# RWKV-6 attention with a gated FFN: one prefix matmul and two exps per unit in the last two super-blocks, permuted FFN units, last output in two halves

## The chip, the cores and the metric

The kernel runs on one core of a Trainium2 chip. Five engines work from their own in-order instruction queues and meet through semaphores: TensorE (PE, matmul), VectorE (DVE), ScalarE (ACT), GpSimd (POOL) and SyncE (SP, which here issues nearly all DMA transfers). The metric is the device time in microseconds (us); 0.5% of it is about 1.06 us.

## What is computed

An RWKV-6 recurrence feeds a gated FFN. B = 4 sequences, H = 8 heads, S = 768 steps, D = 48; then 3072 tokens, d_model = 384, d_ff = 1536.

```python
for t in range(S):                       # state: [B, H, D, D]
    y[:, :, t] = r_t . (state + (u * k_t) v_t^T)
    state = w_t[..., None] * state + k_t v_t^T
x   = y.transpose(0, 2, 1, 3).reshape(B * S, H * D)
xn  = x / sqrt(mean(x * x) + 1e-6) * rms_g
g   = xn @ w_gate
out = (g * sigmoid(g) * (xn @ w_val)) @ w_out          # [3072, 384] float32
```

## The kernel before, in words

**Tiling.** Time is cut into chunks of L = 128 steps, so each sequence has six. Six super-blocks (SB0 to SB5, index m) hold one chunk of each of the four sequences (index j, a *unit*: 128 time steps on the partitions, 384 = 8 x 48 columns). In a step name such as `rk.4.1`, the first number is m and the second j.

**Attention of a unit.** `ln` takes the logarithm of w. `cs` (`cs_mm`, L385) multiplies it by triangular masks: `mask_nge` gives minus the sum of the logs from the own step to the end of the chunk (for r), `mask_gt` gives the sum over the later steps (for k), each 128x384 in a PSUM bank of its own. `exp` (L394) exponentiates both banks in one instruction of 768 elements, and `rk` (L406) multiplies r and k by them. `tr` (PE, SB0 and SB1) or `trp` (a transposing DMA, later) transposes the result; `q` and `qm` (L431, L434) form the masked 128x128 products per head, `y` (L444, L447) multiplies them by v and adds the carried state. `st`, `sn`, `dk`, `dke`, `dm` carry the state on. On the side, POOL computes r*k*u (`ruk1` L472, `ruk2` L476), DVE sums it over a head (`bs` L479), POOL multiplies by v (`yd` L484), and `xa` (L488) adds it to y. `sq` and `rs` (L492, L497) give the RMS factor, `xn` applies it, and `xt`/`xe` (PE transposes and copy) or `xep` (a transposing DMA) lay x down with d_model on the partitions.

**FFN.** `gv` (L532) is one block of a gate (`g`) or value (`v`) product: three matmuls of 512 columns, or six of 256 in SB0 and SB1, where two units form a group. `si` is Silu on the gate block, `hm` (L540) the product with the value block, and `o` (L548) four matmuls of the output product; `oo` copies a finished unit out of PSUM and `od` writes its 128x384 fp32 rows to DRAM. There are twelve blocks of 128 FFN units; `wo[:, f]` has to hold the rows of w_out for block f.

**Weights.** Gate, value and w_out arrive in fp32, once, at the start: 12 loads of 128x768 (`ldw`) and 6 for w_out (`ldwo`, L332), all through seven staging buffers. Each is cast to bf16 in two steps of 384 columns (`wc` L358/L360, with rms_g as scale; `wco`). A load can be issued only when both casts have emptied its buffer. A w_out load brings 256 rows: partition p gets rows p and 128 + p of them, two pieces of 1536 bytes.

**Order.** `PLAN` is a flat list of steps, and the program is that list: each engine executes its steps in the order of the list, and nothing re-orders them. `@n` names a buffer of a ring or a PSUM bank, `/V`, `/A`, `/G` the engine (DVE, ACT, POOL) where there is a choice. ACT changes between two function tables: `tab.le` (ln, exp) at the start of a super-block's exp phase and `tab.si` (Silu) at its end. `warm` steps are matmuls on a constant that fill PE at the start; there are 24.

**What the start of the old order looks like.** SP loads w, k, r of units 0, 1 and 3, then v, and weights in between (w.1, w.3, k.1, w.0, r.0, r.1, k.0, v.0, v.1, gate weight, k.2, ...). All 24 weight casts are on DVE (12) and ACT (12). DVE begins `rk.0 rk.1 vc.0 wc bs.1 bs.0 qm.0 vc.1 qm.1 xa.1 xa.0`, POOL begins `ruk1.1 ruk2.1 ruk1.0 ruk2.0 yd.1 ruk1.2 yd.0`.

`inv_w` (L396) and `r_over_w` (L400) are in the file but no step calls them, and `ONE_SUM`, the tuple of super-blocks that `cs_mm` and `cs_exp` ask for, is empty:

```python
def inv_w(self, m):          # iw = exp(-lw) = 1 / w, all four units
    self.nc.scalar.activation(out=self.iw[:, self.slot["iw", m], :, :, :], in_=self.lw[:, self.slot["lw", m], :, :, 0:D], func=AF.Exp, scale=-1.0)
def r_over_w(self, m, j, eng):   # r = r * iw, in place
    ...
        out=r, in0=r, in1=self.iw[:, self.slot["iw", m], j], op=ALU.mult)
```

Of the kernel before, what the change touches and what calls it, by code (L numbers as in the profile page):

```python
# [24 lines left out]
def bc_mid(ap: bass.AP, n: int, axis: int = 1) -> bass.AP:  # L25
# [22 lines left out]
ONE_SUM = ()  # L48
# [36 lines left out]
    "st": ("st_mm", "stb", 2),  # L85
    "sn": ("st_add", "", 0),
# [7 lines left out]
    "od": ("o_dma", "", 0),  # L94
}
PLAN = """
tab.le.0 ld.0.1.w@0 ld.0.3.w ld.0.1.k@0 ld.0.0.w ld.0.0.r ln.0.1.1@0 ld.0.1.r ldu ln.0.3.1 ld.0.0.k ldg cs.0.3@0
ld.0.0.v@0 ln.0.0.1 ld.0.1.v cs.0.0@2 ldw.1.g@0 cs.0.1@4 exp.0.0 ruk1.0.1@0 ub@6 ld.0.2.k exp.0.1 rk.0.0@0
ldw.5.g@1 exp.0.3 rk.0.1 tr.0.0@7 ube/A ld.0.2.w ruk2.0.1 vc.0.0.1@0/V tr.0.1@6 ld.0.3.r ruk1.0.0@1 tre.0.1@0/A
wc.1.g.1/V ld.0.2.r ruk2.0.0 bs.0.1 tre.0.0/A ld.0.3.k q.0.1@2 yd.0.1@0 bs.0.0 ldw.2.g@2 q.0.0@4 qm.0.1@0  # L100
warm.0@6 ln.0.2.1 ld.0.2.v wc.5.g.1/A vc.0.1.1/V wc.1.g.0/A ldw.4.g@3 qm.0.0@1 st.0.1@7 cs.0.2@2 ruk1.0.2@0
ld.0.3.v y.0.1@4 exp.0.2 yd.0.0@1 y.0.0@5 ldw.0.g@4 xa.0.1@0 warm.1 ruk2.0.2 xa.0.0@1 warm.2 sq.0.1 ldw.2.h@5
rk.0.3@1 warm.3 wc.5.g.0/A rs.0.1 st.0.0@4 warm.4 tab.si.1 bs.0.2 ldw.0.h@6 tr.0.3@5 rk.0.2 yd.0.2@2 warm.5
sq.0.0 wc.4.g.1/V ruk1.0.3@1 warm.6 vc.0.2.1/V xn.0.1@0/A warm.7 wc.4.g.0/A ruk2.0.3 warm.8 ldw.4.h@0
tre.0.3@1/V warm.9 sn.0.1/A warm.10 wc.2.g.0/V rs.0.0 warm.11 ldw.1.h@1 xt.0.1@0 bs.0.3 warm.12 tr.0.2@1
xe.0.1@0/A sn.0.0/V yd.0.3@3 q.0.3@2 wc.0.g.0/A ldw.3.g@3 tre.0.2/V wc.2.h.1/A vc.0.3.1/V q.0.2@4 warm.13
xn.0.0/V wc.0.g.1/A qm.0.2@2 xt.0.0@7 warm.14 wc.2.g.1/A ldw.5.h@4 warm.15 xe.0.0/A ldw.3.h@2 wc.0.h.1/V
wc.2.h.0/V gv.0.0.2.g@0 qm.0.3@0 ldwo.3@5 y.0.2@1 wc.1.h.0/A st.0.2@7 warm.16 st.0.3@4 gv.0.0.0.g@5 wc.1.h.1/A
wc.3.g.0/V wc.3.g.1/A warm.17 ldwo.4@1 wc.4.h.1/V warm.18 gv.0.0.3.g@2 wc.0.h.0/V sn.0.2/A ldwo.0@3 xa.0.2@2
si.0.0.2@0 gv.0.0.4.g@3 wc.5.h.1/V ldwo.1@6 sq.0.2 y.0.3@7 gv.0.0.5.g@1 wc.3.h.1/V si.0.0.0@1 wc.4.h.0/V rs.0.2  # L110
warm.19 sn.0.3/V ld.1.3.w@1 warm.20 gv.0.0.0.v@0 xn.0.2@1/A wco.3.0/G xa.0.3@3 gv.0.0.5.v@5 sq.0.3 ldwo.2@0
hm.0.0.0@0 gv.0.0.1.v@4 si.0.0.3@2 wco.4.0/G ld.1.1.v@1 si.0.0.5@1 xt.0.2@7 warm.21 warm.22 wco.3.1/A warm.23
rs.0.3 gv.0.0.1.g@2 wc.5.h.0/A xn.0.3/V wco.1.1/V wco.0.0/A xt.0.3@0 gv.0.0.2.v@1 wco.0.1/V wc.3.h.0/V ldwo.5@5
xe.0.3/V gv.0.0.4.v@6 hm.0.0.5 gv.0.0.3.v@0 ld.1.1.r@1 xe.0.2/V si.0.0.1@1 gv.0.1.2.g@5 wco.2.1/A hm.0.0.3
ld.1.3.v gv.0.1.1.v@7 hm.0.0.1 si.0.0.4@2 gv.0.1.3.g@2 ld.1.1.k hm.0.0.2 si.0.1.2@1 gv.0.1.0.v@0 wco.1.0/A
ld.1.0.w gv.0.1.0.g@3 wco.5.0/V ld.1.2.w gv.0.1.5.v@1 hm.0.0.4 si.0.1.0@0 gv.0.1.2.v@4 vc.1.1.1@1/A wco.2.0/V
ld.1.1.w wco.4.1/V gv.0.1.1.g@5 hm.0.1.2 ld.1.0.k gv.0.1.5.g@3 hm.0.1.0 si.0.1.1@2 o.0.0.0@6 ruk1.1.1@0 ld.1.0.r
si.0.1.3@1 hm.0.1.1 gv.0.1.4.g@0 si.0.1.5@0 wco.5.1/G ld.1.3.r o.0.0.1 hm.0.1.5 si.0.1.4@2 gv.0.1.4.v@4 ld.1.3.k
vc.1.3.1/V tab.le.1 ruk2.1.1 o.0.0.2 ld.1.2.r gv.0.1.3.v@5 ln.1.1.1@1 oo.0.0@0/V ld.1.0.v o.0.1.0@7 ln.1.0.1
bs.1.1 hm.0.1.4 ln.1.3.1 cs.1.1@2 ruk1.1.0@1 ld.1.2.k o.0.1.1 ln.1.2.1 hm.0.1.3 cs.1.0@0 exp.1.1 ruk2.1.0  # L120
ld.1.2.v o.0.1.2 exp.1.0 rk.1.1@2 o.0.2.0@6 yd.1.1@4 cs.1.2@4 oo.0.1@1/A rk.1.0 dk.1@2 ruk1.1.3@0 exp.1.2
tr.1.1@3 ld.2.0.k@0 cs.1.3@0 dke.1@0 ruk2.1.3 tre.1.1@2/V o.0.3.0@7 exp.1.3 od.0.0 bs.1.0 o.0.3.1 vc.1.0.1/A
rk.1.3@0 ruk1.1.2@1 ld.2.1.v@0 tr.1.0@2 ld.2.1.k o.0.3.2 bs.1.3 dm.1.3/G tre.1.0/A rk.1.2 q.1.1@0 ld.2.0.r
dm.1.1/G vc.1.2.1/A q.1.0@2 qm.1.1@1 tr.1.2@4 oo.0.3@2/A ld.2.2.k dm.1.0/G tr.1.3@5 tre.1.2@0/A qm.1.0@2
ld.2.1.r yd.1.0@0 y.1.1@7 tre.1.3/A yd.1.3@1 od.0.3 xa.1.1@0 y.1.0@4 st.1.2@0 sq.1.1 st.1.0@1 xa.1.0@1
ld.2.1.w@0 q.1.2@2 rs.1.1 ld.3.1.r@1 sq.1.0 q.1.3@4 o.0.2.1 xn.1.1@0/V rs.1.0 qm.1.3@0 xt.1.1@7 o.0.2.2 dm.1.2/G
xn.1.0/A xe.1.1@1/A ruk2.1.2 xt.1.0@4 st.1.3@5 oo.0.2@0/A ld.3.1.k y.1.3@7 xe.1.0/V tab.si.2 gv.1.0.2.v@4
ruk1.2.0@0 xa.1.3@2 ld.2.3.v gv.1.0.0.g@6 sn.1.0 ruk2.2.0 bs.1.2 sq.1.3 gv.1.0.2.g@7 ld.2.2.w sn.1.2 si.1.0.0@0
gv.1.0.1.g@1 rs.1.3 qm.1.2@1 ld.2.2.r si.1.0.2@2 st.1.1@0 yd.1.2@2 gv.1.0.0.v@6 xn.1.3@1/A ld.2.3.w sn.1.3
gv.1.0.3.g@7 hm.1.0.0@1 y.1.2@5 ld.2.0.w si.1.0.3@1 gv.1.0.4.g@2 xa.1.2@3 si.1.0.1@0 ld.2.3.k gv.1.0.1.v@3  # L130
hm.1.0.2 sq.1.2 xt.1.3@5 gv.1.0.5.g@6 ld.2.3.r hm.1.0.1 si.1.0.4@2 rs.1.2 gv.1.0.5.v@7 xe.1.3/V ruk1.2.2@1
si.1.0.5@0 ld.2.2.v gv.1.0.3.v@1 tab.le.2 ld.3.2.w@1 ruk2.2.2 o.1.0.0@4 hm.1.0.3 gv.1.0.4.v@5 ln.2.0.4@0
ld.3.2.k sn.1.1 o.1.0.1 bs.2.2 bs.2.0 ruk1.2.1@1 hm.1.0.4 cs.2.0@2 cs.2.1@0 xn.1.2/G hm.1.0.5 exp.2.0 o.1.1.0@6
ld.2.0.v dk.2@5 exp.2.1 rk.2.0@1 ruk1.2.3@0 o.1.0.2 ld.3.0.w dke.2@1 rk.2.1 xt.1.2@7 cs.2.2@2 ld.3.1.v@1
ruk2.2.1 o.1.1.1 exp.2.2 oo.1.0@2/V cs.2.3@0 trp.2.0@1 xe.1.2/V ruk2.2.3 o.1.1.2 rk.2.2@0 exp.2.3 dm.2.0/G
bs.2.1 tab.si.3 gv.1.1.2.g@5 ld.3.2.r rk.2.3 yd.2.0@3 gv.1.1.1.g@4 si.1.1.2@1 gv.1.1.0.g@7 bs.2.3 dm.2.1/G
od.0.1 si.1.1.1@2 vc.2.0.4@0/V gv.1.1.1.v@2 yd.2.1@4 si.1.1.0@0 trp.2.1@2 gv.1.1.2.v@3 ruk1.3.1@1 gv.1.1.4.g@0
hm.1.1.1 hm.1.1.2 dm.2.2/G ld.3.1.w si.1.1.4@2 q.2.0@4 yd.2.3@0 q.2.1@2 ld.3.3.w gv.1.1.0.v@1 qm.2.0@2 yd.2.2@1
oo.1.1@1/A gv.1.1.3.g@7 ld.3.0.r qm.2.1@0 y.2.0@0 ruk2.3.1 ld.3.2.v gv.1.1.5.g@6 st.2.0@4 xa.2.0@0 q.2.2@2
hm.1.1.0 sq.2.0 sn.2.0 si.1.1.5@1 q.2.3@0 rs.2.0 gv.1.1.5.v@5 qm.2.2@1 si.1.1.3@0 ld.3.0.v dm.2.3/G st.2.3@4  # L140
st.2.2@6 tab.le.3 y.2.1@7 xn.2.0@0/G ld.3.3.v qm.2.3@2 ld.3.3.r ln.3.0.4@1 xa.2.1@1 y.2.3@2 y.2.2@3 ld.4.0.r@0
xa.2.3@2 st.2.1@7 gv.1.1.3.v@0 xa.2.2@3 sq.2.3 ld.3.3.k o.1.2.0@1 sn.2.1 sq.2.2 rs.2.3 sn.2.3 cs.3.3@2 ld.3.0.k
dk.3@7 rs.2.2 sn.2.2 xn.2.3@1/A gv.1.1.4.v@4 sq.2.1 xn.2.2/V hm.1.1.3 xep.2.1@0 dke.3@0 rs.2.1 hm.1.1.4
vc.3.0.4@1/A cs.3.1@6 o.1.3.0@0 xn.2.1/V hm.1.1.5 xep.2.0 o.1.3.1 exp.3.1 o.1.2.1 exp.3.3 rk.3.1@2 cs.3.0@4
ld.4.2.v@0 ruk1.3.0@0 o.1.3.2 exp.3.0 rk.3.3@0 cs.3.2@6 dm.3.3/G o.1.2.2 od.1.1 exp.3.2 rk.3.0 st.3.3@2 dm.3.2/G
st.3.1@3 ld.4.0.v tab.si.4 sn.3.3 st.3.0@4 gv.2.0.3.g@5 dm.3.0/G od.1.0 rk.3.2 gv.2.0.1.g@2 ruk2.3.0 trp.3.0@0
bs.3.1 gv.2.0.5.g@6 si.2.0.1@0 ruk1.3.2@1 gv.2.0.3.v@7 si.2.0.3@2 gv.2.0.1.v@2 trp.3.1@1 oo.1.3@1/A ruk2.3.2
gv.2.0.2.g@5 hm.2.0.1@0 dm.3.1/G gv.2.0.11.g@0 hm.2.0.3 ld.4.0.w@0 oo.1.2@2/A gv.2.0.5.v@2 bs.3.2 si.2.0.5@1
gv.2.0.2.v@1 sn.3.0 si.2.0.11@0 ruk1.3.3@1 ld.4.3.v hm.2.0.5 gv.2.0.4.g@7 si.2.0.2@2 bs.3.0 ruk2.3.3
gv.2.0.8.g@6 ld.4.0.k si.2.0.4@1 sn.3.1 gv.2.0.4.v@0 hm.2.0.2 ld.4.3.k gv.2.0.0.g@4 hm.2.0.4 si.2.0.8@2 ld.4.1.v  # L150
q.3.0@2 bs.3.3 si.2.0.0@1 q.3.1@0 q.3.2@6 qm.3.0@0 ld.4.2.w gv.2.0.0.v@5 gv.2.0.7.g@4 ld.4.1.r qm.3.2@2 y.3.0@2
ruk1.4.0@0 gv.2.0.11.v@3 ld.4.3.w hm.2.0.0 gv.2.0.6.g@6 yd.3.0@2 ld.4.1.w hm.2.0.11 si.2.0.7@1 y.3.2@7
gv.2.0.9.v@5 qm.3.1@1 yd.3.2@3 si.2.0.6@0 od.0.2 gv.2.0.7.v@3 vc.4.0.4@0/A yd.3.1@4 xa.3.2@0 gv.2.0.6.v@4
# [42 lines left out]
class Env:  # L196
# [128 lines left out]
    def cast_w(self, g, w, q, eng):  # L325
        c, f = g // 2, g % 2 * (DF // 2) + q * DM
        dst = (self.wg if w == "g" else self.wv)[:, c, f:f + DM]
        src, sc = self.stage("stage", g, w)[:, q * DM:(q + 1) * DM], self.g_col[:, c:c + 1]
        self.scale(eng, dst, src, sc)
# [278 lines left out]
```

## Time and profile before

| what | value |
|---|---|
| median of 4 runs | 211.59 us (211.39 to 212.76) |
| the profiled execution's own time | 210.71 us |
| its span, first to last instruction | 208.9 us |
| PE busy (matmul) | 190.6 us, 1650 matmuls |
| DVE, ACT, POOL busy | 150.2, 129.5, 105.2 us |
| DMA | 36.74 MB, 130120 packets, mean 176 GB/s |
| TensorE clock granted | full in every slice |

Times in the profile's rows are those of one execution, counted from the start of its span. A duration of a row is one instruction's life; instructions of an engine overlap at their ends, on PE by half, so the distance between two starts is the cost where an engine is full. The chain of work that ended last is followed back from the last instruction to whatever released each step; a wait counts only where it lies on that chain. A landing is the time from issue to the end of a transfer.

### The profile page before, as it was taken

Reading aid. Unit: us, or ns where it says so; the run is one execution under the profiler, and the core shown is the slowest. Engines: PE = TensorE matmul, PEld = TensorE weight load, DVE = VectorE, ACT = ScalarE, POOL = GpSimd, SP = SyncE. Lnnn points to the kernel's source line nnn. Section 1 sums busy time; section 2 is a strip of 40 time slices with the busy share of each in tenths; the row PEclk is TensorE's granted clock in tenths of the full one; section 3 lists DMA queues with packets and bytes.
Section 4 is the critical chain, followed back from the end, with each engine's and each line's share of the span. In section 5 each row is a group of like instructions: output and inputs, shape, how many; then the busy total and the mean of one; then the engine's idle time right before and its main releaser. Section 6 shows DMA issues by size and latency. Waiting matters only on the chain.

```text
span 208.9 us, 4415 instructions
## 1 busy us (share of the span) xinstructions
PE 190.6 (91%) x1650; PEld 117.5 (56%) x1650; DVE 150.2 (72%) x251; ACT 129.5 (62%) x231; POOL 105.2 (50%) x135
## 2 busy tenths in 40 slices
PE   0668699999989999899999999999999999999991
PEld 0244477786769768775455565446654555444560
DVE  2277994877878799998697957799977965042721
ACT  4649867469788977698635976448875354333310
POOL 3176804047787599937919659445399522000000
PEclk9999999999999999999999999999999999999999
DMA  6999999999898979999999999999276007320033
GB/s 133 210 278 281 386 313 301 220 206 222 192 234 164 210 155 221 188 190 195 199 201 216 223 185 239 177 239 235 41 138 141 0 2 67 125 75 2 0 116 115
DMA packets 130120, 36.74 MB, mean 176 GB/s; under 512 B 123953, under 2 KB 128562, under 8 KB 130098
## 3 DMA queue, kind: packets, MB, share of 16 engines
q1 hardware_dynamic: 129696, 36.45, 79.0%
q8 instruction: 13, 0.21, 0.4%
q10 hardware_dynamic: 402, 0.00, 0.1%
q14 instruction: 9, 0.07, 0.1%
HBM read 25.96 MB, written 4.72 MB: 147 GB/s over the span
## 4 chain that ended last, share of the span: by engine, by line
PE 59%; POOL 11%; DVE 10%; DMA 7%; issue 6%; SPq 4%; ACT 3%; POOLq 0%; DVEq 0%; ACTq 0%
PE ps L532 34%; PE ps L548 17%; SPq L298 4%; POOL ruk L472 3%; DMA stage_x<-in_moe_w_out_dram 3%; POOL ydr L484 3%; DVE qts L434 3%; POOL ruk L476 2%; PE ps L385 2%; DVE rkA L406 2%; DMA in_w<-in_w_dram 2%; DMA in_rk<-in_k_dram 2%; PE ps L431 2%; POOL st L466 1%; PE ps L447 1%
## 5 line engine op out<-in xcount | busy, mean ns | idle before, releaser
L536 ACT ACTIVATE sg<-ps 128x512 bf16<-128x512 f32 x72 | 41.0, 595 | 41.3 <-PE ps L532 23.6
L540 DVE TENSOR_TENSOR ht<-ps,sg 128x512 bf16<-128x512 f32 x72 | 47.5, 683 | 17.2 <-PE ps L532 12.0
L532 PE MATMUL ps<-xnt,wv 128*128 128x256 bf16 (+1 forms) x288 | 55.0, 326 | 0.5 <-DVE wv L360 0.5
L532 PE MATMUL ps<-xnt,wg 128*128 128x256 bf16 (+1 forms) x288 | 54.8, 326 | 0.1
L548 PE MATMUL ps<-wo,ht 128*128 128x384 bf16 x288 | 53.8, 326 | 0.0
L472 POOL TENSOR_TENSOR ruk<-in_rk 128x384 f32<-128x384 f32 x24 | 24.3, 1012 | 34.7 <-DMA in_rk<-in_k_dram 12.0
L548 PEld LDWEIGHTS <-ht 128*128 128x128 bf16 x288 | 27.3, 98 | 18.0 <-issue 0.3
L532 PEld LDWEIGHTS <-wg 128*128 128x128 bf16 x288 | 27.3, 98 | 17.8 <-issue 0.4
L532 PEld LDWEIGHTS <-wv 128*128 128x128 bf16 x288 | 27.0, 98 | 17.6 <-DVE wv L360 0.8
L406 DVE TENSOR_TENSOR rkA<-in_rk,ps 128x768 bf16<-128x768 f32 x24 | 22.4, 949 | 10.6 <-ACT ps L394 10.6
L434 DVE TENSOR_TENSOR qts<-ps,mask_lt 128x1024 bf16<-128x1024 f32 x24 | 28.6, 1214 | 0.4 <-PE ps L431 0.4
L497 POOL TENSOR_TENSOR rstd<-rstd,mhalf 128x1 f32<-128x1 f32 x24 | 13.4, 563 | 23.6 <-ACT junk L492 23.4
L476 POOL TENSOR_TENSOR ruk<-ruk,u_bc 128x384 f32<-128x384 f32 x24 | 24.1, 1007 | 2.2 <-ACT u_bc L354 1.1
L394 ACT ACTIVATE ps<-ps 128x768 f32<-128x768 f32 x24 | 18.5, 795 | 6.2 <-PE ps L385 5.6
L484 POOL TENSOR_TENSOR ydr<-in_v,diag 128x384 f32<-128x384 f32 x24 | 20.4, 860 | 2.7 <-DVE diag L479 2.6
L466 POOL TENSOR_TENSOR st<-sf,wcr 128x384 bf16<-128x384 f32 x19 | 15.5, 832 | 1.9 <-ACT wcr L378 1.9
L488 DVE TENSOR_TENSOR xb<-ps,ydr 128x384 bf16<-128x384 f32 x24 | 13.0, 550 | 4.5 <-PE ps L447 2.4
L341 ACT ACT_TABLE_LOAD x12 | 15.4, 1283 | 0.9 <-PEq L592 0.7
L492 ACT ACTIVATE junk<-xb 128x388 bf16<-128x388 bf16 x24 | 12.6, 524 | 4.6 <-DVE xb L488 4.1
L350 DVE COPY obr<-ps 128x384 f32<-128x384 f32 x11 | 6.1, 553 | 12.1 <-PE ps L548 12.0
L385 PE MATMUL ps<-lw,mask_nge 128*128 128x384 bf16 x24 | 8.5, 355 | 6.5 <-ACT lw L344 6.4
L479 DVE TENSOR_REDUCE diag<-ruk 128x8 f32<-128x384 f32 x24 | 12.9, 544 | 0.4 <-POOL ruk L476 0.4
(71 smaller groups left out, 190.6 us busy)
## 6 DMA issues: line engine op xcount, KB each, us to landing
in_w<-in_w_dram SPq DMA_DIRECT2D x24, 192.0 KB, 3.7
in_rk<-in_k_dram SPq DMA_DIRECT2D x24, 192.0 KB, 3.7
in_rk<-in_r_dram SPq DMA_DIRECT2D x24, 192.0 KB, 3.9
in_v<-in_v_dram SPq DMA_DIRECT2D x24, 192.0 KB, 4.0
out_dram<-obr SPq DMA_DIRECT2D x24, 192.0 KB, 3.0
ht<-in_moe_w_gate_dram SPq DMA_DIRECT2D x5, 384.0 KB, 5.0
stage_x<-in_moe_w_val_dram SPq DMA_DIRECT2D x3, 384.0 KB, 4.8
ht<-in_moe_w_val_dram SPq DMA_DIRECT2D x3, 384.0 KB, 5.8
```

Source lines behind the costliest of these rows:

```text
L341: self.nc.scalar.preload_act_table_set(LN_EXP if kind == "le" else SILU)
L394: self.nc.scalar.activation(out=ps, in_=ps, func=AF.Exp)
L406: self.nc.vector.tensor_tensor(out=self.half("rkA", m, j)[:, :, :, 0:D], in0=self.in_rk[:, self.slot["in_rk", m], j], in1=self.b2(("cs", m ...
L434: self.nc.vector.tensor_tensor(out=self.qts[:, self.slot["qts", m, j]].rearrange("p a q t -> p (a q) t"), in0=self.b2(("qb", m, j)).rearra ...
L466: (self.nc.vector if eng == "DVE" else self.nc.gpsimd).tensor_tensor(out=self.st[:, m % 2, j].rearrange("p q (a d) -> p q a d", a=2), in0= ...
L472: self.nc.gpsimd.tensor_tensor(out=self.ruk[:, self.slot["ruk", m, j]], in0=rk[:, 0], in1=rk[:, 1], op=ALU.mult)
L476: self.nc.gpsimd.tensor_tensor(out=t, in0=t, in1=self.u_bc, op=ALU.mult)
L484: self.nc.gpsimd.tensor_tensor(out=self.ydr[:, self.slot["ydr", m, j]], in0=self.in_v[:, self.slot["in_v", m], j], in1=self.diag[:, m * SB ...
L532: self.nc.tensor.matmul(ps[:, a * n:(a + 1) * n].rearrange("p (u t) -> p u t", t=L), lhsT=w[:, c, f * 128:(f + 1) * 128], rhs=x[:, :, c], ...
L536: self.nc.scalar.activation(out=self.sg[:, self.slot["sg", m, g, i]], in_=self.b1(("gvb", m, g, i, "g")), func=AF.Silu)
L540: self.nc.vector.tensor_tensor(out=self.ht[:, self.slot["ht", m], fs[0]:fs[-1] + 1, t0:t0 + n], in0=self.b1(("gvb", m, g, i, "v")).rearran ...
L548: self.nc.tensor.matmul(ps, lhsT=self.ht[:, self.slot["ht", m], f, j * L:(j + 1) * L], rhs=self.wo[:, f, :], start=(f == 0), stop=(f == FC ...
```

## The change

1. `ONE_SUM = (4, 5)`: in SB4 and SB5 a unit has one prefix matmul (`mask_gt`) instead of two. `cs_exp` takes two exps of it, one with scale -1 and one with scale +1, 384 elements each. The first is the factor of r times w, so two new steps go with it: `iw` (`inv_w`, once per super-block, on ACT inside the exp phase) and `rw` (`r_over_w`, once per unit, in place in r, after `ruk1` of that unit has read it and before its `rk`).
2. The FFN units are permuted. A cast takes every second column of a staging buffer (384 of them, step 8 bytes), so that blocks of even and of odd units arise; partition p of a w_out load gets rows 2p and 2p + 1 of its 256, one piece of 3072 bytes; `cast_wo` puts the two halves at the matching blocks.
3. The last unit's output (`5.2`) is copied in two column halves, one by ACT and one by DVE, and written by two DMAs of 768-byte rows, one from ACT's queue and one from SP's.
4. `PLAN` is a new list. Every engine's order differs from the start on.

```diff
-ONE_SUM = ()
+ONE_SUM = (4, 5)
 OPS = {
+    "iw": ("inv_w", "iw", 1),
+    "rw": ("r_over_w", "", 0),
+    "ooh": ("o_out_half", "obr", 2),
+    "odh": ("o_dma_half", "", 0),
     def cast_w(self, g, w, q, eng):
-        c, f = g // 2, g % 2 * (DF // 2) + q * DM
-        dst = (self.wg if w == "g" else self.wv)[:, c, f:f + DM]
-        src, sc = self.stage("stage", g, w)[:, q * DM:(q + 1) * DM], self.g_col[:, c:c + 1]
-        self.scale(eng, dst, src, sc)
+        c, n = g // 2, DF // 2
+        dst = (self.wg if w == "g" else self.wv)[:, c, g % 2 * n:(g % 2 + 1) * n].rearrange("p (c i x) -> p c i x", c=2, x=128)
+        src = self.stage("stage", g, w).rearrange("p (i x c) -> p i x c", c=2, x=128)
+        self.scale(eng, dst[:, q], src[:, :, :, q], self.g_col[:, c:c + 1])
     def load_wo_hw(self, i):
-        self.nc.sync.dma_start(out=self.stage_o(i), in_=self.wout[i * 256:(i + 1) * 256, :].rearrange("(c p) m -> p c m", p=128))
+        self.nc.sync.dma_start(out=self.stage("stage_o", i), in_=self.wout[i * 256:(i + 1) * 256, :].rearrange("(p c) m -> p (c m)", c=2))
     def cast_wo(self, i, c, eng):
-        self.copy(eng, self.wo[:, 2 * i + c], self.stage_o(i)[:, c])
+        self.copy(eng, self.wo[:, i // 3 * 6 + c * 3 + i % 3], self.stage_o(i)[:, c])
+    def o_out_half(self, m, j, h):
+        x = slice(h * DM // 2, (h + 1) * DM // 2)
+        self.copy("DVE" if h else "ACT", self.obr[:, self.slot["obr", m, j], x], self.b1(("ob", m, j))[:, x])
+    def o_dma_half(self, m, j, h):
+        row0, x = j * 768 + m * L, slice(h * DM // 2, (h + 1) * DM // 2)
+        (self.nc.sync if h else self.nc.scalar).dma_start(out=self.out[row0:row0 + L, x], in_=self.obr[:, self.slot["obr", m, j], x])
```

The new order, by queue, at the places that matter:

```
start, SP:   w.0 k.0 w.1 r.3 r.1 w.3 k.1 v.1 [gate 2] r.0 w.2 r.2 v.0 k.3 [gate 1] [gate 0] [gate 5] [val 1] k.2 v.2 ...
start, DVE:  wc.2.g.1 ube rk.1 rk.0 bs.1 rk.3 bs.0 wc.1.g.1 qm.1 wc.5.g.0 xa.1 vc.0 qm.0 qm.3 rk.2 xa.0 tre.2 bs.3 wc.0.h.0 wc.2.h.1 wc.5.h.1 wc.3.g.0 xe.1 xe.0 ...
start, POOL: ruk1.0 ruk1.1 ruk2.0 ruk2.1 yd.0 yd.1 ruk1.3 rs.1 ruk2.3 wc.1.g.0 wc.5.g.1 yd.3 rs.0 wc.4.h.0 ruk1.2 ruk2.2 wc.2.h.0 ...
start, PE:   ... xt.0.0 warm x4 gv.0.0.5.g gv.0.0.4.g warm st.0.3 gv.0.0.3.g ...
SB4, ACT:    tab.le ln.4 iw.4 sq.3.3 exp.4.0 dke.4 exp.4.1 vc.4 exp.4.3 exp.4.2 tab.si
SB5, ACT:    tab.le ln.5 iw.5 sq.4.1 sq.4.2 sq.4.3 exp.5.3 xn.4.3 dke.5 oo.3.2 exp.5.2 oo.3.1 exp.5.1 exp.5.0 tab.si
end, PE:     gv.5.0.10.g gv.5.0.10.v o.5.1.0 gv.5.0.9.v o.5.3.0 o.5.1.1 o.5.0.0 o.5.1.2 ... o.5.2.2, then ooh x2, odh x2
```

Weight casts are now 10 on DVE, 10 on ACT and 4 on POOL (1.g, 5.g, 4.h, 2.h; `g` is gate, `h` is value). Of the eight `rw`, five are on DVE and three on POOL. SB0's u broadcast (`ube`) moves from ACT to DVE.

## The prediction, made before the changed kernel ran

> **What bounds the kernel now.** I first read busy time in stretches of the run (us, then busy us and instruction count by engine, granted clock, DMA share, GB/s).
>
> ```profile
> core 0: us, PE busy (x) PEld busy (x) DVE busy (x) ACT busy (x) POOL busy (x), PEclk, DMA share, GB/s
> 0.00:10.00 10.00, 3.81 (x8) 1.25 (x8) 2.13 (x11) 5.03 (x7) 3.00 (x13) 1.00 0.89 172
> 10.00:20.00 10.00, 7.59 (x63) 4.34 (x63) 7.51 (x12) 6.45 (x12) 6.94 (x8) 1.00 1.08 274
> 20.00:30.00 10.00, 7.80 (x84) 5.42 (x85) 10.00 (x19) 7.88 (x17) 4.74 (x6) 1.00 1.01 351
> ...
> 80.00:100.00 20.00, 18.61 (x221) 13.29 (x219) 18.18 (x27) 15.55 (x28) 14.76 (x19) 1.00 0.98 197
> 100.00:120.00 20.00, 19.81 (x167) 10.47 (x164) 17.30 (x28) 12.67 (x22) 12.59 (x15) 1.00 1.04 210
> 120.00:140.00 20.00, 20.00 (x141) 10.44 (x140) 15.38 (x25) 11.14 (x21) 12.41 (x14) 1.00 1.09 210
> 140.00:160.00 20.00, 20.00 (x193) 11.63 (x192) 16.80 (x28) 15.12 (x27) 13.54 (x17) 1.00 0.69 148
> ```
>
> There are two regimes. From 38 us TensorE (PE) is nearly full: idle is 0.54 us in 38-60, 0.46 in 60-80, 1.39 in 80-100, 0.19 in 100-120 and none afterwards, 2.6 in all. Before 38 us it is not. In 20-30 it seems 78% busy, but part of that is the `warm` filler (24 matmuls, 0.216 us each, 5.2 us together), and VectorE (DVE) has no gap. The clock is full throughout, so it plays no part. I then read the chain of work that ended last (start, duration, what).
>
> ```profile
> 29.46 0.67 DVE wv L360 x2
> 30.13 0.02 issue
> 30.14 6.46 DMA stage_x<-in_moe_w_out_dram
> 36.60 0.02 issue
> 36.62 0.63 DVE wo L350 x2
> 37.25 0.34 DVE wv L360
> 37.59 0.05 issue
> 37.64 7.27 PE ps L532 x65
> ...
> 198.17 6.51 PE ps L548 x40
> ...
> 204.75 0.48 ACT obr L354
> ```
>
> Up to 37.64 the chain is DMA and casts, then PE, then one output copy that ends at 205.23, and 3.7 us of writing out (span 208.93). The time is therefore (moment at which PE becomes full) + (PE work left) + (PE idle later) + (tail), and I cost the change in these four terms.
>
> **PE work.** SB4 and SB5 each lose four `mask_nge` prefix matmuls. In the timeline the two of a unit start 0.163 us apart (121.28, 121.45, 121.61), so eight give 1.30 us. They lie where PE is full (121-125 and 146-154), so all of it counts: **-1.30**. The group's mean of 355 ns must not be used: it is one instruction's life in an overlapped pipeline.
>
> **What SB4/SB5 pay for it.**
> - ScalarE (ACT): two `iw` of 1536 elements; nearest row is `ln` at 1.48 us. Eight units take two exps of 384 instead of one of 768: 2 x 0.48 (the 384-element PSUM copy) less 0.80, so +0.17 each. Together 4.3 us, half in each exp phase (table load to table load). SB4's phase also takes over a 1.47 us value cast. In the old SB4 phase (117.39-127.65) ACT idles 1.06 + 0.35, and 1.79 before its second silu: 3.2 us of cover against 1.48 + 0.68 + 1.47 = 3.6. SB5's phase idles 0.26 + 0.66 + 1.10 + 0.66 = 2.7 against 1.48 + 0.68 + one output copy 0.48 = 2.6. PE does not need ACT at once: the new plan gives it twelve `o` blocks (7.8 us), prefix and `dk` matmuls and five or six gate/value blocks (0.65 each) before it needs a silu, about 13 us, against my queue sums of 12 to 13 us for ACT. I take **0**; if the cover is gone it costs up to 1 us a phase.
> - `r/w`: five on DVE (0.55, the nearest row is the 384-element `st` multiply), three on POOL (1.01, the `ruk` row): 2.8 and 3.0 us. In 100-160 DVE idles 10.5 us of 60 and POOL 21. They must follow `ruk1` of their unit and precede `rk`; what waits behind a late one is `rk`, its exp banks and the next prefix matmul. **0**, bounds 0 and +1.
>
> **w_out in 3072-byte rows.** The Trainium skill (DMA: Bandwidth & Descriptors, Specifications) puts the least size for line rate at 512 B, so 1536 against 3072 B would be worth nothing. The trace disagrees:
>
> ```profile
> 22.00:24.00 2.00, 1.89 (x24) 1.14 (x22) 2.00 (x3) 1.70 (x4) 1.92 (x3) 1.00 1.03 396
> 24.00:26.00 2.00, 0.39 (x12) 0.23 (x8) 2.00 (x6) 1.63 (x3) 1.34 (x2) 1.00 1.05 412
> ...
> 30.00:32.00 2.00, 2.00 (x26) 1.72 (x24) 2.00 (x7) 1.50 (x4) 0.60 (x1) 1.00 0.90 300
> 32.00:34.00 2.00, 2.00 (x19) 1.69 (x18) 1.19 (x3) 1.81 (x5) 0.51 (x1) 1.00 0.84 270
> ```
>
> Gate and value weights (3072 B rows) move at 396-412 GB/s, w_out (1536 B) at 270-300. For the 2.36 MB of w_out that is 5.9 instead of 8.3 us, part of it only because the queue is less full (0.84-0.90). I use it: 1.05 us per w_out load instead of 1.4, so 1.3 to 2.4 us of queue time. On the path it is worth what the plan makes of it, below.
>
> **Permuted casts and the new start.** Weight casts now read every second fp32. On DVE, contiguous ones take 0.41; without the two-per-cycle mode I bound them by 0.61 (384 elements at the 1 ns slope between rows). The skill (VectorE: DVE Perf Modes, What auto-detection actually checks) makes that mode depend on memory and dimensions, not on step; I take 0.41. Four casts go to POOL, where no such row exists: its fp32-to-bf16 copy took 0.51, its bf16 tensor-scalar 1.255, and twice that, 2.5, if the wider strided source halves it. I take 1.25.
>
> The whole start is re-ordered, so I lay it out by queue. Loads landed at 3.6, then one per 0.9 us (192 KB) or 1.05 us (384 KB). In the new order r of unit 0 is tenth, behind one weight: 12.2 us (before it was fifth, 7.6). POOL then runs two `ruk1` and two `ruk2` at 1.0: 16.3. DVE, in order, waits for that: `bs`, `rk.3`, `bs`, cast, `qm` (0.47, 0.87, 0.47, 0.33, 1.15) to 19.6; cast and `y`, then `xa.0.1` to 20.7; `vc`, two `qm`, `rk.2`, `xa.0.0` (0.3, 2.3, 0.87, 0.47) to 24.7; `tre`, `bs.3` to 26.0. POOL meanwhile: `yd`, `yd`, `ruk1`, `rs`, `ruk2` to 23.2, two weight casts to 25.7, `yd.3` (waits for `bs.3`) to 26.8, `rs.0.0` to 27.4. Then `xn` 0.6, transposes 0.3, `xe` 0.35: the first gate matmul can start at 28.8, against 27.13 before, **+1.67**.
>
> From there, before: 61 of the 256-column matmuls at 0.109, 8 warms, two each of `y`, `st`, `xt`, and about 1.0 us of waiting, until 37.64. After: the same warms, one `y` and one `st` fewer (-0.37), and by my queue sums almost no waiting (-0.95): gates are cast by 30.8, values by 33, the three w_out casts on DVE wait for landings at 35 to 36, two blocks before PE needs the banks behind them. I reach twelve blocks at 39.2, where the old schedule would stand at 30.97 + 12 x 0.656 = 38.84: **+0.35**. The faster w_out rows are already in this; at 1.4 us a load those landings come 1 us later.
>
> **Later idle.** All the rest of the order is new too, and the 2.6 us of idle are a property of the old order. I found no stall by queue sums in the exp phases of SB4 and SB5. Nor is there one in the last twelve blocks: the last `hm` is ready 0.5 us before `o.5.1.2` needs it. For 38-120 I cannot say: **0**, with -2 to +2.
>
> **Tail.** The last copy becomes two of 192 columns on ACT and DVE: 0.35 (DVE's 0.55 less 192 elements at about 1 ns) instead of 0.48, **-0.13**. The store becomes two, on ACT's queue and SP's. The skill (DMA: Bandwidth & Descriptors, Issuing engines are not separate DMA queues) says both run on the same 16 engines and only issue time is saved: by that rule 0 of the 3.7 us. By the row, if the movement (192 KB at 300 GB/s, 0.6 us) were halved, -0.3. I take -0.12 between them, **-0.25** with the copy.
>
> **Sum.** 208.93 - 1.30 + 0.35 + 0 - 0.25 = 207.73 of span. The profiled execution took 210.71, 1.78 above its span: 209.5. The runs' median of 211.59 lies 0.88 above that execution: **210.4**.
>
> **Rivals.**
> - *The new order also removes idle.* The 1.39 us in 80-100 came from a late k load of SB3 (chain: landing at 95.5, `rk`, `st`), and SB3's loads are ordered anew; with -2 there the result is 208.4. For it: a single late load made most of it. Against it: POOL gets more work. 0.20.
> - *Slower: the POOL casts hold up the first FFN block.* `wc.1.g.0` and `wc.5.g.1` stand ahead of `yd.3` and `rs.0.0` on POOL, with 0.3 us of slack. At 2.5 us each they add 2.2 us to the start, PE has nothing but warms, and the result is 212.6; with strided DVE casts at 0.61 on the same path (five before `xe`), 213.4. The gain is eaten from 1.25 + (1.2 + 0.3)/2 = 2.0 us a cast. For it: DVE is busy throughout and the POOL rows next to busy DVE grow (1.18 for 1.00). 0.25.
> - *The matmuls go, but the time stays:* ACT's exp phases become the bound at 0.6 us each, or idle in 38-120 grows by 1.2: 211.6. 0.10.
> - Forecast, 210.4 with its own range 209.3-211.5: 0.45.
>
> About 0.5% (1.06 us: below 210.53, above 212.65) is what a measurement of this kernel can tell from no change. The forecast's own range falls a little over half below 210.53 (0.26); with the first rival 0.46 faster; the slower rival and the forecast's upper edge give 0.24 slower; 0.30 between. The range, 207.9 to 213.2, takes in both rivals' centres.
>
> **What would show it.** Right: 24 + 16 matmuls on the two prefix masks; the first L532 matmul near 28.8; w_out loads spaced near 1.05 us; POOL fp32 weight casts near 1.25; the exp phases longer by 2-3 us with PE at 20.00 of 20; the last copies near 0.35. Wrong: POOL casts above 2 us, the first gate matmul after 30 us, PE idle above 3 us between 40 and 120, or a first silu of SB3 or SB4 that PE waits for.

## The result, and the profile after

| | before | after |
|---|---|---|
| median | 211.45 us (63 runs) | 210.83 us (44 runs) |
| range | 209.88 to 213.89 us | 208.74 to 212.99 us |
| the profiled execution | 210.71, span 208.9 us | 211.20, span 209.3 us |

The ratio is 0.9954, 95% interval [0.994, 0.9968]: about 1.0 us faster, where the medians differ by 0.6 us and the forecast was 210.4. The ratio is of the means of the runs that lie within 1.5% of the fastest of their kernel, which leaves out 8 of the 44 of after and 3 of the 63 of before. The profiled execution of before lies 0.7 us below its median and that of after 0.4 above, so the two spans must not be subtracted. Differences of one part are taken from timed runs with intervals, and the traces only say where.

First the same stretches of the run as were shown of before (us, busy us and instruction count by engine, clock, DMA share, GB/s).

```profile
core 0: us, PE busy (x) PEld busy (x) DVE busy (x) ACT busy (x) POOL busy (x), PEclk, DMA share, GB/s
20.00:30.00 10.00, 6.61 (x82) 3.86 (x81) 8.67 (x16) 8.19 (x18) 7.02 (x8) 1.00 1.04 307
...
120.00:140.00 20.00, 20.00 (x155) 10.99 (x154) 16.56 (x29) 15.56 (x27) 12.85 (x15) 1.00 1.06 199
140.00:160.00 20.00, 19.98 (x178) 11.40 (x176) 17.81 (x30) 17.11 (x33) 17.55 (x21) 1.00 0.69 153
```

The two regimes are still there. In the exp phases of SB4 and SB5 (120 to 160) PE is full, though ACT has 32.7 us of work in them instead of 26.3. The start is thinner: VectorE is busy 8.67 us of 10 between 20 and 30 us, where it had no gap before. PE's idle time after 38 us is 3.3 us (0.71, 0.25, 0.90, 1.39 and 0.02 in the stretches from 38 on) against 2.6.

Next the chain of work that ended last, from the start of the second regime to the end.

```profile
28.60 6.00 DMA ht<-in_moe_w_val_dram
...
35.65 0.94 POOL ydr L489
...
205.88 0.37 DVE obr L355
206.25 0.02 issue
206.27 0.32 ACT obr L359
```

Where before a w_out load led to PE at 37.64, now a value weight that lands at 34.6 and POOL's `yd` of unit 0.2 do, and PE runs from 37.23 on. The two halves of the last output stand one behind the other.

Of the new work, the exp of 384 and the weight cast on POOL, in the groups by shape (instruction count, then busy us and mean ns):

```profile
L396 ACT ACTIVATE ps<-ps 128x384 f32<-128x384 f32 x8 | 3.8, 475 | 0.4 <-PE ps L390 0.2
...
L365 POOL TENSOR_SCALAR wg<-ht,g_col 128x384 bf16<-128x384 f32 x2 | 2.5, 1270 | 0.0
```

Those prices were met: the exp of 384 took 0.475 (forecast 0.48), `r/w` 0.56 and 1.10 (0.55 and 1.01), the weight cast on POOL 1.27 (1.25). A strided DVE cast took 0.42 where nothing lay beside it (forecast 0.41).

### The profile page after: what moved, and what is told of

Read it like the earlier page. It is cut to its first block, busy times and chain, and to the rows that moved or that the text cites. A ratio compares the mean times of both kernels' runs of the same rounds, so it can differ in the third digit from the quotient of the medians.

```text
span 209.3 us, 4422 instructions
## 1 busy us (share of the span) xinstructions
PE 187.9 (90%) x1642; PEld 116.4 (56%) x1642; DVE 149.4 (71%) x248; ACT 136.4 (65%) x244; POOL 116.7 (56%) x144
## 4 chain that ended last, share of the span: by engine, by line
PE 68%; DMA 8%; SPq 7%; DVE 7%; ACT 4%; issue 2%; POOL 1%; DVEq 0%; ACTq 0%; POOLq 0%
PE ps L537 39%; PE ps L553 20%; SPq L302 5%; DMA in_v<-in_v_dram 3%; DMA ht<-in_moe_w_val_dram 3%; DMA rkT<-rkA 3%; DVE qts L439 2%; PE ps L390 2%; PE ps L436 2%; DVE xb L493 2%; SPq L327 2%; DVE rkA L411 2%; PE ps L452 1%; PE ps L449 1%; ACT rkT L359 1%
## 5 line engine op out<-in xcount | busy, mean ns | idle before, releaser
L541 ACT ACTIVATE sg<-ps 128x512 bf16<-128x512 f32 x72 | 41.3, 598 | 33.2 <-PE ps L537 26.6
L537 PE MATMUL ps<-xnt,wv 128*128 128x256 bf16 (+1 forms) x288 | 55.9, 326 | 1.0 <-DVE xb L493 0.3
L537 PE MATMUL ps<-xnt,wg 128*128 128x256 bf16 (+1 forms) x288 | 53.7, 326 | 0.0
L502 POOL TENSOR_TENSOR rstd<-rstd,mhalf 128x1 f32<-128x1 f32 x24 | 13.9, 581 | 22.6 <-ACT junk L497 22.4
L471 POOL TENSOR_TENSOR st<-sf,wcr 128x384 bf16<-128x384 f32 x17 | 14.6, 867 | 4.4 <-ACT wcr L383 4.4
L359 ACT COPY obr<-ps 128x384 f32<-128x384 f32 (+1 forms) x15 | 7.0, 467 | 12.5 <-PE ps L553 9.9
L493 DVE TENSOR_TENSOR xb<-ps,ydr 128x384 bf16<-128x384 f32 x24 | 12.8, 550 | 3.2 <-POOL ydr L489 1.9
L399 ACT ACTIVATE ps<-ps 128x768 f32<-128x768 f32 x16 | 12.3, 794 | 2.7 <-PE ps L390 2.6
L349 ACT ACTIVATE lw<-in_w 128x384 bf16<-128x384 f32 (+1 forms) x12 | 9.8, 838 | 4.3 <-DMA in_w<-in_w_dram 4.3
```

Source lines behind the costliest of these rows:

```text
L471: (self.nc.vector if eng == "DVE" else self.nc.gpsimd).tensor_tensor(out=self.st[:, m % 2, j].rearrange("p q (a d) -> p q a d", a=2), in0= ...
L493: self.nc.vector.tensor_tensor(out=self.xb[:, self.slot["xb", m, j], 0:DM], in0=self.b1(("yb", m, j))[:, 0:DM], in1=self.ydr[:, self.slot[ ...
L537: self.nc.tensor.matmul(ps[:, a * n:(a + 1) * n].rearrange("p (u t) -> p u t", t=L), lhsT=w[:, c, f * 128:(f + 1) * 128], rhs=x[:, :, c], ...
L541: self.nc.scalar.activation(out=self.sg[:, self.slot["sg", m, g, i]], in_=self.b1(("gvb", m, g, i, "g")), func=AF.Silu)
```

## Experiments

Three measures from the traces recur below. **First gate matmul** is the start of the first `gv`. **Twelve blocks** is the start of the last of the 72 matmuls of 256 columns that make up the first twelve FFN blocks, plus its cost of 0.11 us. **Rest** is PE's end less that moment. Each is of one execution: the rest of after is 164.1 and that of the same kernel in the control 166.5, so differences of 2 us between two rests say nothing. Ratios are to the kernel before, timed alongside on the same chip.

### The new order with one part taken out

*Control: the kernel after as it is.*

> The changed kernel again, unaltered, for a second execution of it in the profile. Theory A (the start of the new order costs about 2.9 us, the rest gains it back): the first gate matmul lies at 29.5 to 30.5 us again, twelve FFN blocks are done at 41 to 42.5, the last PE instruction to the end of the span takes 3.3 to 3.6 us. Theory B (the profiled execution was an unlucky one and the start costs about 0.4 us as predicted): twelve blocks done at 39 to 40.

*Two prefix sums again, in the new order.*

```diff
-ONE_SUM = (4, 5)
+ONE_SUM = ()
 (PLAN: the two iw and eight rw steps are left out)
```

> The changed kernel with two prefix matmuls and one wide exp in SB4 and SB5 again, no iw, no r/w; everything else in the new order. If the eight matmuls lie on a full PE and nothing else there binds, it is 1.3 us slower than the changed kernel. If ScalarE's longer exp phases had eaten the gain, it is equal to it or faster.

*One copy and one store at the end.*

```diff
-ooh.5.2.1@0 ooh.5.2.0 odh.5.2.0 odh.5.2.1
+oo.5.2@0/A od.5.2
```

> The changed kernel with the last unit copied by ScalarE and stored by SP in one piece. By the prediction's tail term it is 0.25 us slower than the changed kernel. By the two traces alone (PE's end to span's end 4.25 us before, 3.45 after) 0.8 us slower. If the two halves only run one after the other, as the trace has them (0.36 and 0.32 us), and a transfer's end doesn't depend on its size, equal or up to 0.2 us faster.

*w_out in rows of 1536 bytes.*

```diff
-self.wout[i * 256:(i + 1) * 256, :].rearrange("(p c) m -> p (c m)", c=2)
+self.wout[i * 256:(i + 1) * 256, :].rearrange("(c p) m -> p c m", p=128)
```

> The changed kernel with w_out loaded in two pieces of 1536 bytes per partition again; the rows then lie in the wrong FFN blocks, so this part of the computation is changed, with the same instructions. If row length sets the rate (400 against 280 GB/s), the w_out loads take 0.4 us more each and 1 to 2 us more together, and the kernel is 0.5 to 1 us slower. If 512 bytes are enough for full rate, equal.

This run leaves out the matching of w_out rows to FFN blocks, so its output differs; the instructions are the same.

| run | median, us | ratio, 95% interval | first gate matmul | twelve blocks | rest |
|---|---|---|---|---|---|
| control | 212.55 | 0.9970 [0.9938, 1.0003] | 30.8 | 41.1 | 166.5 |
| two sums | 214.25 | 1.0057 [1.0021, 1.0092] | 30.7 | 41.8 | 167.4 |
| one store | 212.22 | 0.9968 [0.9932, 1.0005] | 30.7 | 41.1 | 163.9 |
| short rows | 212.70 | 0.9973 [0.9942, 1.0004] | 31.4 | 42.1 | 165.3 |

The single prefix sum is worth 1.0057 - 0.9970 = 0.87% or 1.85 us, with about 1 us on either side when the two intervals are combined. It carries the whole gain: with two sums the new order is 0.57% (1.2 us) slower than before. The halved store (0.9970 against 0.9968) and the long rows (0.9970 against 0.9973) are worth nothing that can be measured.

### The old order with one part put in

*The two halves alone; the permutation with the long rows alone.* The edits are the diff's own.

> The kernel before with the last output in two halves alone. Prediction's term: 0.25 us faster than before. Reading the two traces alone: 0.8 us faster. Halves one after the other and a transfer's end independent of its size: equal.

> The kernel before, in its own order, with the permuted FFN units and w_out in rows of 3072 bytes alone. If row length sets the rate, the w_out load that the chain waits for (issue 30.14, landing 36.6) lands about 1 us earlier, and the kernel is 0.3 to 1 us faster. If strided casts cost 0.2 us more each on VectorE (12 of them), the start is up to 2 us slower. If neither, equal.

*One sum in the old order.* The r*k products of units 4.3 and 5.0 had to come before their `rw`, so they moved ahead, into a third buffer.

```diff
-ONE_SUM = ()
+ONE_SUM = (4, 5)
 (PLAN, SB4)
-ln.4.0.4@0 ... exp.4.1 ruk1.4.1@1 rk.4.0@1 ... rk.4.1 ... exp.4.3 ... rk.4.2
+ln.4.0.4@0 iw.4@0 ... exp.4.1 ruk1.4.1@1 rw.4.0/V rk.4.0@1 ... rw.4.1/V rk.4.1 ... ruk1.4.3@2 rw.4.3/G exp.4.3 ... rw.4.2/V rk.4.2 ruk2.4.3
```

> The kernel before, in its own order, with one prefix matmul and two exps in SB4 and SB5 alone (the ruk steps of units 4.3 and 5.0 moved ahead of their rk, into a third buffer). If the eight matmuls are what counts: 1.3 us faster than before. If the order must be made anew to hide the longer exp phases: 0 to 1 us slower than before, with PE idle in 120-130 and 150-158.

*All three in the old order.*

> The kernel before, in its own order, with all three parts. Theory A (the new order's start costs 2.9 us, later idle gives back 0.4): the sum of the parts without that cost, 2 to 3 us faster than before and 1 to 2 us faster than the changed kernel. Theory B (the new order is neutral): about 1 us faster than before, equal to the changed kernel. If the exp phases bind in the old order: no faster than before.

*Only the moved products and the third buffer, with two sums.* This is the control of the one-sum run.

> The kernel before with two prefix sums in every unit, as it was, and only the two r*k products of units 4.3 and 5.0 moved ahead, into a third buffer, as the one-sum run in the old order had to have them. That run was 4.4% slower than before. Theory (the old order has no room on VectorE and ACT for the inverse, the r/w products and the second exp): this control is within 0.3% of before, ratio 0.998 to 1.003, and the 9.4 us belong to the new work. Rival (moving the products on GpSimd, and the sums that wait for them, did it): ratio 1.01 to 1.045.

| run | median, us | ratio, 95% interval |
|---|---|---|
| halves | 212.32 | 1.0004 [0.9977, 1.0031] |
| permutation and long rows | 212.56 | 1.0018 [0.9985, 1.0051] |
| one sum | 221.84 | 1.0443 [1.0394, 1.0492] |
| all three | 220.94 | 1.0376 [1.0326, 1.0425] |
| moved products alone | 212.42 | 0.9997 [0.9962, 1.0031] |

The halves and the rows are worth nothing here either. The surprise is the single sum, which takes eight matmuls away and costs 4.4% (9.4 us). The control with the moved products is at 0.9997, so the loss belongs to `iw`, `rw` and the second exp. The windows of the one-sum run say where it lies:

```profile
120.00:140.00 20.00, 16.52 (x100) 8.35 (x98) 14.31 (x22) 12.23 (x22) 13.34 (x14) 0.91 0.78 141
140.00:160.00 20.00, 18.98 (x186) 10.80 (x185) 17.72 (x30) 13.26 (x26) 7.35 (x10) 1.00 0.83 177
```

PE is idle 3.5 and 1.0 us in these stretches, where it was full before, and another 3.1 us from 160 to 180. The clock falls to 0.91 in the first: eight output matmuls that begin at 129.66, behind waits of 1.62 and 1.19 us, took 2.77 us instead of 1.46. The chain in SB5's exp phase shows the mechanism:

```profile
162.85 1.00 POOL in_rk L400
...
163.87 0.97 DVE rkA L404
...
168.07 5.93 DMA rkT<-rkA
```

`rw` (L400) and, from 160.51 on, the products that must precede it stand in front of `rk` (L404). `rk` frees the banks of the next prefix matmul (PE waited 5.0 us in four places for it) and releases the transposing DMA, which takes 5.9 us. `rw` is not alone in it: in SB4, `iw` on ACT stands in front of the square of another unit, and VectorE (2.6 us) and POOL (3.0 us) wait for what follows from that square. So `iw`, `rw` and the second exp are not separated here, and this is one placement of them in the old order; others were not tried. In the new order most `ruk1` and `rw` stand ahead of their exp, and PE has output and gate blocks queued in front of what needs them: in the trace of after it waits 0.7 us for `rk` from 38 to 160 us.

### The start of the new order

By then the start stood out as the mis-sized term: over the five traces of the new order above (after among them) the first gate matmul comes at 30.1 to 31.4 instead of 28.8 and the twelve blocks at 41.0 to 42.1 instead of 39.2. My theory was that late loads do it, the value weight of the chain above and r of unit 0.0.

*The late value weight issued earlier.*

```diff
-sq.0.0 wc.5.g.1/G ldw.4.h@1 ... wc.0.g.0/A ... ldw.3.h@2
+wc.0.g.0/A sq.0.0 wc.5.g.1/G ldw.3.h@2 ldw.4.h@1 ...
```

> The kernel after, with two steps moved in the start: the ACT cast that empties a staging buffer (gate weight 0, first half) ahead of the square of unit 0.0 that it stood behind, and the value weight 3 load, which waits for that buffer, ahead of the value weight 4 load. In the profile after, this load was issued at 28.60, landed at 34.6, and VectorE waited 2.91 us for it at 34.6. Theory (the start lost 1.8 us instead of the forecast's 0.35, and part of that is this late load): the load lands 2 to 4 us earlier, the wait is gone, the twelve blocks of the first FFN group are done 0.5 to 1.0 us earlier than after (41.6 in the mean of five runs of that order, so 40.6 to 41.1), and the ratio to before is 0.992 to 0.995 against 0.997. Rival (the whole weight stream limits, so another load becomes the late one, value weight 4 first): twelve blocks still at 41.3 to 42, ratio 0.996 to 0.999.

*In addition r of unit 0.0 two loads earlier, and the first weight cast on DVE behind `rk`.*

```diff
-ld.0.1.v@0 ldg cs.0.1@2 ldw.2.g@0 exp.0.1 ld.0.0.r ... wc.2.g.1/V ... ube/V rk.0.1@0 ruk1.0.0@0 ldw.1.g@1 rk.0.0
+ld.0.0.r ld.0.1.v@0 ldg cs.0.1@2 ldw.2.g@0 exp.0.1 ... ube/V ... rk.0.1@0 ruk1.0.0@0 ldw.1.g@1 rk.0.0 wc.2.g.1/V
```

> As the run before, and r of unit 0.0 is loaded two places earlier (ahead of v.1 and of the first gate weight), with the first DVE weight cast moved behind the two r, k products and the u copy ahead of it, so that neither GpSimd nor VectorE waits for that weight. Theory (the first gate matmul came at 30.1 to 31.4 instead of 28.8 because GpSimd's products started at 12.8 and VectorE had no gap from then on): r lands about 1.5 us earlier, VectorE's first head sum starts at 15.2 instead of 16.7, the first gate matmul at 28.6 to 29.5, the twelve blocks are done at 39.5 to 40.5, and the ratio to before is 0.986 to 0.991. Rival (the weight stream or VectorE's own sum of work decides the start): first gate matmul at 30 or later, ratio 0.994 to 0.998.

*In addition the last output product in two PSUM banks.*

```diff
+if (m, j) == (5, 2):   # per f and half h, 192 columns into bank 3 or 6
+    self.nc.tensor.matmul(self.last(h)[:, x], lhsT=..., rhs=self.wo[:, f, x], ...)
```

> As the run before, and the output product of the last unit is made in two column halves in two PSUM banks (24 matmuls of 192 columns instead of 12 of 384), so that the two copies of the tail need not run one after the other as they did after (VectorE 205.88 to 206.24, ACT 206.27 to 206.59). Theory (the forecast's 0.13 us for the copy were lost because ACT waited for VectorE): the two copies overlap, PE's end to the end of the span is 3.1 us instead of 3.45 to 3.5, PE's work grows by at most 0.3 us for the shorter matmuls, and the ratio equals the run before within 0.001. Rival (the stores alone set the tail): copies overlap but the tail stays at 3.4 to 3.6. The start is that of the run before in both, so its first gate matmul and twelve blocks are a second reading of it.

| run | median, us | ratio, 95% interval | first gate matmul | twelve blocks | rest |
|---|---|---|---|---|---|
| early value weight | 213.41 | 1.0050 [1.0013, 1.0086] | 30.7 | 42.2 | 166.4 |
| and early r | 213.53 | 1.0005 [0.9960, 1.0050] | 31.5 | 42.7 | 164.9 |
| and two banks | 213.06 | 1.0013 [0.9977, 1.0048] | 30.5 | 41.5 | 166.5 |

The theory fell. The value weight did come earlier and VectorE's 2.9 us of waiting for it were gone, but the kernel got no faster. r of unit 0.0 came 2 us earlier too (in the run with the early r, POOL's first product began at 10.71 instead of 12.78), and this is what VectorE did with it in the two-banks run, which has the same start:

```profile
14.36 0.55 DVE L479 TENSOR_REDUCE diag<-ruk 128x8 f32<-128x384 f32 x1 [0.89 <-POOL ruk L476]
16.93 0.95 DVE L406 TENSOR_TENSOR rkA<-in_rk,ps 128x768 bf16<-128x768 f32 x1 [2.02 <-DMA in_rk<-in_k_dram]
```

The number in brackets is the wait before the instruction. The first head sum starts 2.3 us earlier (14.36 for 16.66), and then VectorE waits 2.02 us for k of unit 0.3 and reaches that product at 16.93, where after reached it at 17.13. In the run with the early r it was 17.87, behind a wait of 2.62 us. That load has the same loads in front of it in both orders, only in another sequence, and the DMA engines have no free share here (1.02 and 1.04 in the windows of after). So the load that moved gains only until the next one that did not.

In the second half of the start, PE itself tells what it waited for. Between the first gate matmul and the twelve blocks the forecast has 10.4 us. The control and the one-store run take 10.3, without a wait; the other six take 10.7 to 11.7, with 0.2 to 0.9 us of waiting. First the wait of the run with the early value weight, then the last one of after:

```profile
36.34 1.38 PE L533 MATMUL ps<-xnt,wv 128*128 128x256 bf16 x11 [0.82 <-POOL wv L361]
```

```profile
37.23 0.81 PE L537 MATMUL ps<-xnt,wv 128*128 128x256 bf16 x6 [0.34 <-DVE xb L493]
```

In all three runs of this section PE waits once, for POOL's second value-weight cast (0.82, 0.76 and 0.60 us). Moving value weight 3 ahead made value weight 4 the late one: POOL's cast of it starts at 31.6, 32.1 and 30.9, and in the five other traces at 30.1 to 30.7. That is the rival of the expectation, though twelve blocks at 42.2 and a ratio of 1.005 are worse than it said. In after the 0.81 us are in part two casts (0.29 and 0.17), and the rest is `xa` of unit 0.2. POOL's rows of after show that unit's `yd`:

```profile
30.11 1.28 POOL L365 TENSOR_SCALAR wv<-ht,g_col 128x384 bf16<-128x384 f32 x1 [1.77 <-DMA ht<-in_moe_w_val_dram]
...
33.63 1.27 POOL L365 TENSOR_SCALAR wv<-ht,g_col 128x384 bf16<-128x384 f32 x1
35.65 0.93 POOL L489 TENSOR_TENSOR ydr<-in_v,diag 128x384 f32<-128x384 f32 x1 [0.75 <-DVE diag L484]
```

Two fp32 weight casts stand in front of it, but both were done at 34.9, and it waited another 0.75 us for its head sum, which stood in VectorE's queue behind the late value weight. So three different waits make up this half in the eight traces, each below 1 us. They do not explain all of the early value weight's 0.5%: its trace has 1.4 us more PE idle after 38 us than that of after, which I did not follow up.

The two banks did what was asked of the copies:

```profile
207.96 0.32 ACT L354 COPY obr<-ps 128x192 f32<-128x192 f32 x1 [2.07 <-PE ps L550]
208.04 0.36 DVE L350 COPY obr<-ps 128x192 f32<-128x192 f32 x1 [0.76 <-PE ps L550]
```

They overlap and end 0.38 us after PE (208.02 to 208.40). After needed 0.73 us (205.86 to 206.59), where ACT's copy began only as VectorE's ended, and one whole copy before took 0.55 (204.68 to 205.23). But from the last copy to the end of the span it then took 3.5 us. With two stores this stretch is 2.7 us in after and 3.7 and 4.1 in the two runs above; with one store it is 3.7 in before and 3.0 in the one-store run. The landing of the last store sets the tail, its spread is larger than the gain, and the runs show no gain from halving it. None of these three runs beats the kernel after, which against before stands at 0.9954 and 0.9970 above, though they were not timed side by side with it.

## Why the prediction was right, and which of its steps failed

The forecast was 1.2 us faster, and about 1.0 us was measured (0.6 by the medians and in the control). The sign and the cause are right: the eight matmuls pay, and in the new order the exp phases have cover. The sizes of the terms are less good:

| term of the sum | forecast | measured |
|---|---|---|
| PE work | -1.30 us | -1.85, about 1 us either way (two sums against control) |
| new start | +0.35 us | +1.2 together with rows, halves and later idle (two sums against before, +0.4 to +2.0) |
| later idle | 0 | +0.7 in the two profiled executions |
| tail | -0.25 us | nothing measurable (halves 1.0004 in the old order, 0.9968 against 0.9970 in the new) |

- **PE work.** 16 `mask_nge` matmuls are left, and the price of 0.163 us each lies inside the interval. What the single sum takes in the exp phases was hidden, as said. They grew by 1.3 us (SB4) and 0.4 us (SB5), less than the 2 to 3 forecast. The one-sum run in the old order shows how much the order matters for this: there the cover is missing, and my bound of "up to 1 us a phase" would have been far too low (9.4 us over two phases).
- **New start: mis-sized.** r of unit 0.0 let POOL begin at 12.8 instead of 12.2, and `xa` of unit 0.0 ended at 25.2 where the sums had 24.7: 0.5 us late so far. The later steps lost another 0.8. `tre` had a wait of 0.32 and a copy of 0.69. POOL waited 1.2 us for a square on ACT, so its two casts ended at 26.6 instead of 25.7 and `rs` of unit 0.0 at 28.4 instead of 27.4. And PE's order has four `warm` matmuls (0.86 us) between the last transpose and the first gate matmul, of which I had counted only what the copy takes (0.35). Hence 30.1 in after instead of 28.8. "By my queue sums almost no waiting" after that was right in two of the eight traces and short by up to 0.9 us in the others. The slower rival had POOL's casts hold up the first block, at more than 2 us a cast; they took the expected 1.27 us.
- **How much the start costs.** Against the trace of before the twelve blocks come 2.2 to 3.2 us later, more than the timed 1.2. But that trace is the best one of its order: the five others of the old order have a lower clock at the start (last section) and reach twelve blocks at 39.4 to 40.6, 40.1 in the mean, against 41.55 in the mean of the five of the new. The difference of about 1.4 us, an estimate from these traces, fits the timed 1.2.
- **w_out rows: no worth.** The step "1.05 us per w_out load instead of 1.4" failed. From 34 to 42 us, where most of w_out arrives, after moved 229, 305, 325 and 206 GB/s, the short-row run 229, 225, 299 and 251. That is no clear difference, and the ratio shows none. In after the third w_out load stood 4.0 us in SP's queue for its buffer (the releaser that the profile names is a square on ACT), so the order of ACT's steps spaced these loads, not only their rate. The old order shows it without such a wait, from 30 to 34 us in before and then in the run with the long rows:

```profile
DMA packets 783, 1.14 MB, mean 285 GB/s; under 512 B 45, under 2 KB 779, under 8 KB 783
```

```profile
DMA packets 416, 1.13 MB, mean 282 GB/s; under 512 B 49, under 2 KB 49, under 8 KB 416
```

Packets of 1536 and of 3072 bytes moved at the same rate. So the row that I read as an effect of row length has another cause; that the queue is less full there (0.84 to 0.90) is part of it, and the rest is open. The Trainium skill's 512-byte rule (DMA: Bandwidth & Descriptors, Specifications), which I had set aside for the row, agrees with the runs.
- **Tail: failed in both terms.** The two copies took 0.18 us longer in after than the one of before, and the store's "-0.12 between them" should have been the skill's 0.
- **Later idle.** 3.3 us against 2.6 in one execution each. In the other traces of the new order as it was forecast it is 2.7, 4.3, 4.9 and 5.1, two of them beyond the +2 that I had allowed; traces of the old order that keep its SB4 and SB5 have up to 3.35.
- **Signs.** Two of the four signs of being wrong came true: the first gate matmul came after 30 us in all traces of the new order, and PE was idle for more than 3 us between 40 and 120 in most of them (3.25 in after). Of the signs of being right, the first gate matmul and the w_out spacing failed, and the exp phases grew by less than said. The others came.

So errors went in opposite directions: start and tail cost about 1.1 us more than summed and the single sum brought about 0.5 more, each within its interval of uncertainty. That the total is so near is in part luck. The rival with less idle did not happen.

## What to carry to other kernels

Removing work from the bounding engine pays only where the work that replaces it has a place in every queue it is put into. The same edit was worth -0.87% in an order made for it and +4.4% in one that was not, where the new instructions stood in front of the one that frees PE's banks. When a start is fed by a saturated load stream, moving one load forward gains only until the next load that did not move, and it can make the one that it passed late. So sum the whole stream and follow each unit to the last step before PE, fillers in PE's own queue included.

## What the runs showed of the hardware

**The granted clock is not always full at the start.** I had written that it plays no part. Before and the run with the halves have the same steps up to 28 us and nearly the same times, and in both PE is nearly idle from 24 to 26 us (0.39 and 0.40 us busy). First 28 to 30 us of before, then 26 to 30 us of the run with the halves:

```profile
28.00:30.00 2.00, 2.00 (x27) 1.55 (x24) 2.00 (x4) 2.00 (x5) 0.00 (x0) 1.00 0.87 261
```

```profile
26.00:28.00 2.00, 1.86 (x16) 1.07 (x11) 2.00 (x5) 0.51 (x2) 0.00 (x0) 0.76 1.02 368
28.00:30.00 2.00, 2.00 (x22) 1.55 (x20) 1.38 (x3) 1.12 (x3) 0.00 (x0) 0.50 0.85 231
```

The third number from the right is the clock. In the run with the halves it fell to 0.50 as the FFN began, and the first six gate matmuls took 1.44 us instead of 0.81. The four others of the old order have this dip as well (0.72 in the mean of 26 to 32 us in all five), while of the eight of the new order one has a dip at the start (0.90 and 0.81) and one at 108 to 112 us (0.67), behind a PE wait of 1.9 us. The Trainium skill (TensorE: Matmul & The Clock Gate, What's actually happening) describes a gate between half and full rate that is set by PE's activity in a free-running window of about 3.4 us. The half rate and the chance from run to run agree with the rows. But its rule of thumb of no idle gaps over about 3.4 us (HAM oscillation) is too mild here: the longest gap before these dips was 1.6 us, with 0.4 us of matmuls on its far side. A part of the gain of the new order is probably that it meets this dip less often. The record has the mean clock of the timed runs: it was full (0.999 or more) in 24 of 56 runs of after and its control and in 14 of 93 of before, and there typically 0.992. In before, full-clock runs were 0.6 to 0.9 us faster than the others, so the dip accounts for about 0.2 us of the gain, an estimate from these figures; the 63 runs of before in the main comparison have no clock on record. The gain of the single sum is not touched: the control has 0.994 in the mean and the run with two sums 0.9935.

**VectorE can be held up by POOL.** The strided weight cast took 0.42 us alone (at 11.80 in after), and 1.16 us at 13.62 in the run with the early r, beside POOL's `ruk2`. `rw` on VectorE took 0.56 us in after and 1.26 us at 126.92 in the one-sum run of the old order, beside POOL's `ruk2`. In both cases VectorE's instruction began after POOL's and ended 0.2 to 0.4 us after POOL's end. A cast at 35.52 in the run with the early value weight took 0.41 us beside a weight cast on POOL (34.99 to 36.28), so not every pair does this.
